# Layer B's transform of time split as 64 by 32, with square transposes on VectorE and matrix products in parts of the array, in a four-layer FFT kernel

## The chip, the cores and the metric

The kernel runs on one core of one Trainium2 chip. The metric is the device time of one whole execution in microseconds. The kernel before was run three times: median 890.2 us, from 884.12 to 890.73.

## The reference

The state `x` has 2048 rows (time `l`) of 512 channels (`d`), float32. Two kinds of layers follow each other, A, B, A, B, each adding to `x` what it makes of the row-normed `x` (LayerNorm without weights).

```python
def A(x, w_r, w_i):                       # a filter in the 2-D spectrum
    X = rfft2(x, axes=(-2, -1))           # 2048 x 512
    return irfft2(X * (w_r + 1j * w_i), s=(2048, 512))

def B(u, A_re, ..., log_dt, Dskip):       # a causal convolution over time, per channel
    dt = exp(log_dt)[:, None]
    P = exp((dt * (A_re + 1j * A_im))[:, :, None] * l)     # 512 x 128 x 2048
    K = einsum("dn,dnl,dn->dl", C, P, dt * Bc).real        # kernel: 512 x 2048
    y = irfft(rfft(u.T, 4096) * rfft(K, 4096))[:, :2048]   # zero-padded
    return y.T + u * Dskip

x = x + A(norm(x)); x = x + B(norm(x)); x = x + A(norm(x)); x = x + B(norm(x))
```

The weights of the two layers A are the same, and so are those of the two layers B, so the kernel `K` and its spectrum are made once.

## The kernel before

Everything is float32 matrix products with tables of sines and cosines, apart from parts of the making of `K`. `x` stays in SBUF as 128 partitions of 16 rows; partition `p` holds rows `16p` to `16p+15`.

**The planner.** Each piece of work is a Python generator (`forward_b`, `group_b`, and so on). A `yield` names the engine and the buffers that the next instructions need and the marks that must have been set. `Clock` simulates the engines with a table of costs (`COST`), takes the ready piece of the lowest rank, and so writes one static order for each engine. Ranks are in the plans `plan_k`, `plan_a` and `plan_rest`. There are two runs of the planner: the first holds the making of `K` and the first layer A, the second all that follows.

**Layer A** is four steps: `forward_a` (norm L505 or L507, sums on POOL L531, products L546 and following, copy), the groups `first_a` and `group_a` in the spectrum (loads of `G`, products, weights), `inv_a` (products L724, copy, product L733, copy, sums on POOL and DVE L744 to L754, new row statistics), and `spread` (ACT square root L490, DVE reciprocal L492), which hands the statistics of four rows on.

**Layer B, before.** The transform of 4096 points is odd-frequency (it carries the zero padding), and splits time as 128 by 16: a product over the 128 partitions, then small transforms over 16. `forward_b` works on two of the 16 rows and half of the channels (`e`): a norm on DVE (L507), eight products with the table `Rb` (L774), two copies on ACT (L776), and a DMA from SBUF to SBUF (L792) that puts the 32 columns of a group beside each other in `place`. `group_b` does one of 16 groups: it loads the kernel's spectrum `khat` (L858) or makes it from `yk`, takes the small transform by products (L804, L805, 32 records), multiplies complex numbers on DVE (L867, twice 128x512) and POOL (L873, twice 128x256), turns back by products (L880), and copies on ACT (L886). `inv_b` moves the rows back by DMA (L895), does the product over time with `RbT` (L902), adds to `x` on DVE (L908), and then either takes the row statistics (L916, L918) or stores a piece of the output (L924, on ACT's queue). In the plan, layer B's forward pieces stand among the inverse pieces of the layer A ahead of it, and layer A's forward pieces among the last pieces of layer B.

**The kernel `K`, before.** `unit_k` builds it 16 channels at a time in 32 units; its last products (L1088) leave 128x256 in PSUM, and two DVE copies (L1099) put them into `KS`. `store_k` writes `KS` to DRAM, `turn_k` reads it back transposed, takes the product over time (L1132), copies on ACT (L1137) and writes `yk`; `spectra_k` makes half of the spectra ahead of layer B, and `group_b` the other half on its first pass.

## Time and profile before

| | |
|---|---|
| median of 3 runs | 890.2 us |
| profiled execution: its span | 887.0 us |
| PE (matrix products) busy | 691.0 us, 78% of the span |
| DVE busy | 565.2 us, 64% |
| ACT busy | 429.1 us, 48% |
| POOL busy | 372.6 us, 42% |
| DMA | 138.22 MB, 156 GB/s in the mean |

The profiled execution is one execution; its span runs from its first to its last instruction, 3.2 us less than the median of the runs.

How to read it: a row of the groups names line, engine, operation, `out<-in` by the program's names, partitions x elements, and a count, then the busy time, the mean of one in ns, and the idle time just before them with what ended it. For a PE row, `128*32` is the part of the array, rows by columns, that a product uses. A product of two float32 operands is two records (`x2048` records are 1024 products). PEld are the loads of the stationary operand, which run beside the products. A row of the timeline has a start in us, a duration, an engine, what it did, and in brackets the idle time before it with what ended that.

### The profile page before, as it was taken

How to read it: one execution, taken by the hardware profiler on the slowest of the kernel's cores; microseconds unless marked ns; L12 is line 12 of the kernel's file. 1: busy time of each engine (PE TensorE's matmuls, PEld its weight loads, DVE VectorE, ACT ScalarE, POOL GpSimd, SP SyncE). 2: the span in 40 equal slices, each digit the busy share in tenths (PEclk: the TensorE clock that was granted, in tenths of full speed). 3: DMA queues.
4: the chain of work that ended last, by engine and by line, in shares of the span. 5: the costliest groups of instructions: out<-in, count | busy, mean ns of one | idle time of the engine just before them, and what ended most of it. 6: DMA issues, size and time to landing. Idle time of an engine off the chain costs nothing. (4 is left out here: it accounts for less than half of the span.)

```text
span 887.0 us, 18504 instructions
## 1 busy us (share of the span) xinstructions
PE 691.0 (78%) x7208; PEld 478.4 (54%) x7208; DVE 565.2 (64%) x1086; ACT 429.1 (48%) x805; POOL 372.6 (42%) x419
## 2 busy tenths in 40 slices
PE   0048767978999888846899989799877897499967
PEld 0046554746666543425556755688755454266746
DVE  6988787546948587692444544586876888265522
ACT  2447677477777867644244213165542454122110
POOL 0047655235536466560234215164443645065430
PEclk9999789979999798988899989799999999799998
DMA  9043003523523844568978993810641067747938
GB/s 332 21 147 95 13 27 130 160 79 110 154 83 114 301 146 144 191 232 175 243 189 239 265 357 124 195 37 15 237 168 42 22 155 186 211 122 186 263 94 226
DMA packets 91862, 138.22 MB, mean 156 GB/s; under 512 B 6812, under 2 KB 61344, under 8 KB 91136
## 3 DMA queue, kind: packets, MB, share of 16 engines
q1 hardware_dynamic: 59520, 107.68, 41.0%
q10 hardware_dynamic: 32256, 29.37, 11.6%
q8 instruction: 57, 0.93, 0.4%
q14 instruction: 29, 0.24, 0.1%
HBM read 76.34 MB, written 27.13 MB: 117 GB/s over the span
## 5 line engine op out<-in xcount | busy, mean ns | idle before, releaser
L873 POOL TENSOR_TENSOR wk<-wk 128x256 f32<-128x256 f32 x128 | 89.2, 727 | 172.9 <-DVE wk L867 169.7
L867 DVE TENSOR_TENSOR wk<-ps,wk 128x512 f32<-128x512 f32 x128 | 79.8, 684 | 91.3 <-PE ps L805 47.3
L1075 POOL TENSOR_TENSOR Y<-wk,Y 128x1024 f32<-128x1024 f32 x32 | 77.0, 2406 | 84.1 <-ACT wk L1063 57.3
L774 PE MATMUL ps<-wk,cRb 128*64 128x256 f32 x512 | 67.7, 406 | 23.1 <-DVE wk L507 23.1
L902 PE MATMUL ps<-wk,cRbT 64*128 64x256 f32 x512 | 68.2, 411 | 15.7 <-DMA wk<-Ya 13.4
L880 PE MATMUL ps<-wk,Y 64*128 64x256 f32 x512 | 73.6, 405 | 2.9 <-POOL wk L873 2.9
L546 PE MATMUL ps<-cRa,wk 128*128 128x128 f32 x128 | 27.6, 300 | 56.9 <-POOL wk L531 56.9
L902 PEld LDWEIGHTS ps<-wk,cRbT 64*128 64x128 f32 x512 | 55.4, 203 | 27.7 <-issue 14.2
L774 PEld LDWEIGHTS ps<-wk,cRb 128*64 128x64 f32 x512 | 46.0, 146 | 44.9 <-DVE wk L507 23.1
L776 ACT COPY wk<-ps 128x512 f32<-128x512 f32 x64 | 37.4, 586 | 62.8 <-PE ps L774 52.6
L531 POOL TENSOR_TENSOR wk<-wk 128x256 f32<-128x256 f32 x32 | 25.0, 780 | 89.3 <-DVE wk L507 55.3
L880 PEld LDWEIGHTS ps<-wk,Y 64*128 64x128 f32 x512 | 43.8, 185 | 32.9 <-POOL wk L873 25.4
L1060 DVE SCALAR_TENSOR_TENSOR wk<-wk,ps 128x1024 f32<-128x1024 f32 x32 | 38.8, 1212 | 33.0 <-ACT wk L1058 33.0
L908 DVE TENSOR_TENSOR x<-x,ps 128x256 f32<-128x256 f32 x64 | 24.8, 408 | 54.6 <-PE ps L902 54.4
L507 DVE TENSOR_SCALAR wk<-x,mv,rs 128x256 f32<-128x256 f32 (+1 forms) x80 | 40.9, 550 | 22.4 <-issue 12.5
L1028 PE MATMUL ps<-wk,Y 96*128 96x512 bf16 x128 | 44.1, 425 | 13.5 <-DVE Y L1071 7.7
L546 PEld LDWEIGHTS ps<-cRa,wk 128*128 128x128 f32 x128 | 21.5, 208 | 58.9 <-POOL wk L531 58.0
L1044 ACT ACTIVATE Y<-ps 128x1024 f32<-128x1024 f32 x48 | 46.9, 1030 | 9.8 <-PE ps L1028 9.1
L1088 PE MATMUL ps<-Y 128*32 128x64 f32 x2048 | 41.9, 244 | 10.1 <-POOL Y L1076 8.2
L1088 PEld LDWEIGHTS ps<-Y 128*32 128x32 f32 x2048 | 36.3, 126 | 24.8 <-POOL Y L1076 13.5
L886 ACT COPY Ya<-ps 128x256 f32<-128x256 f32 x64 | 20.5, 376 | 57.5 <-PE ps L880 55.1
L1071 DVE TENSOR_TENSOR Y<-ps,Y 128x1024 f32<-128x1024 f32 x32 | 39.0, 1218 | 13.5 <-ACT ps L1064 13.5
(218 smaller groups left out, 1802.4 us busy)
## 6 DMA issues: line engine op xcount, KB each, us to landing
wk<-khat SPq DMA_DIRECT2D x48, 256.0 KB, 3.0
yk<-wk ACTq DMA_DIRECT2D x32, 256.0 KB, 3.3
wk<-yk SPq DMA_DIRECT2D x32, 256.0 KB, 3.9
khat<-wk ACTq DMA_DIRECT2D x32, 256.0 KB, 5.4
Y<-in_cGb_dram SPq DMA_DIRECT2D x32, 256.0 KB, 6.0
wk<-Y SPq DMA_DIRECT2D x16, 512.0 KB, 8.9
wk<-Ya SPq DMA_DIRECT2D x16, 512.0 KB, 4.6
Y<-in_W_dram SPq DMA_DIRECT2D x12, 515.0 KB
```

The costliest lines, as they stand in the source:

```text
L507: self.nc.vector.tensor_scalar(xn, self.x[:, s2, d], m, r, op0=OP.subtract, op1=OP.mult)
L546: nc.tensor.matmul(o, pq[:, 0, :], self.Ra, start=True, stop=False)
L774: self.nc.tensor.matmul(p[64 * s:64 * s + 64, 256 * h:256 * h + 256], self.Rb[:, 2 * h + j, :], xn[s], start=True, stop=True)
L867: nc.vector.tensor_tensor(t[c], X[:, c, None, :].to_broadcast([128, 2, 256]), k, op=OP.mult)
L873: nc.gpsimd.tensor_tensor(Z[:, c], t[0][:, c], t[1][:, c], op=op)
L880: nc.tensor.matmul(v[j], gi[o, 2 + c, :], Z[o, c, :], start=c == 0, stop=c == 1)
L902: nc.tensor.matmul(q[s], self.RbT[o, i, :], y[o, i, :], start=i == 0, stop=i == 3)
L1028: self.nc.tensor.matmul(p, f[:, c:c + 128], self.oh[:k, o:o + 512], start=True, stop=True)
L1044: nc.scalar.activation(m[:, :, 1024:] if i == 2 else m[:, i, :1024], p.rearrange("p (i m) -> p i m", i=2) if i == 2 else p, AF.Exp)
L1071: nc.vector.tensor_tensor(E[:, 1, :1024], p, m[:, :1024], op=OP.mult)
L1075: nc.gpsimd.tensor_tensor(E[:, 0, :1024], c, m[:, :1024], op=OP.mult)
L1088: nc.tensor.matmul(pk[32 * j:32 * j + 32, 64 * e:64 * e + 64], E1[:, r, i, :], E2[:, r, i], start=r == 0, stop=r == 1)
```

## The change

Layer B's time is split as 64 by 32 in place of 128 by 16. `x` now has partition `64h + p` hold rows `32p + 16h` to `32p + 16h + 15`, so each load of `x` and each store is two DMAs of 64 partitions (`lines`).

- `norm_b`: the 16 norms of a layer B are on ACT (L497, 128x512), into `Ya`; `NORMS` puts those of the second layer A there too.
- `forward_b`, 16 pieces of 32 channels: two products (L781) that use 64 rows of the array each, then one DVE transpose in squares of 32 by 32 (L784, 128x1024, from PSUM) that writes into `P` the order that the DMA made before.
- `step_b`, 16 pieces in place of 32 of `group_b`: in the first layer a load of `yk` (L808), the kernel's spectrum (16 products, L792), a copy on ACT (L814) and a store of `khat` (L815), in the second layer a load of `khat` (L804); then the spectrum (16 products on 64 rows by 32 columns, L792), a product on DVE of 128x1024 (L825), a copy on ACT of 128x512 (L828), a product on POOL of 128x1024 (L832), 32 products on 32 rows by 64 columns (L840, eight parts of the array), which also do the sums that POOL did before, and two copies on ACT (L846).
- `inv_b`, 8 pieces of 64 channels: a DVE transpose 128x2048 in SBUF (L855), four products of 512 columns (L861), one addition of 128x1024 on DVE (L866). The output leaves in 8 DMAs of 512 KB with runs of 512 bytes on SP's queue (L871). `stats_b` holds the row statistics.
- `rows_k`, 8 pieces, replaces `store_k`, `turn_k` and `spectra_k`: an addition of `Dskip` on POOL, two times four products (L1079) and a transpose (L1083), a store of 1 MB. In `unit_k` one copy on ACT (L1061) replaces the two copies of L1099.
- The plan has four runs, one per layer (`stage`), with buffers and PSUM banks of their own. Layer B's forward pieces no longer stand among layer A's inverse, nor layer A's forward among layer B's end.

```diff
--- before.py
+++ after.py
@@ -11,38 +11,36 @@
+RINGB1 = {"pk": (1024, 3), "kh": (1024, 3), "t0": (1024, 2), "t1": (1024, 2), "xi": (512, 2)}
+RINGB2 = {"kh": (1024, 6), "t0": (1024, 2), "t1": (1024, 2), "xi": (512, 2)}
+RINGP = {"iy": (2048, 4)}
+BANKSB = {'u': (0, 2), 'v': (4, 6)}
...
-NORMS = False, False, True, False
+NORMS = False, True, True, True
...
@@ -759,169 +751,139 @@
-    def turn_b(self, xn, y, kinds):
-    def forward_b(self, r, b, e, st):
-    def rows(self, b, e):
-    def spectra_k(self, q):
-    def tables(self, r):
-    def group_b(self, r, q, e):
-    def inv_b(self, r, b, e, st=None):
...
+    def norm_b(self, r, s2, st):
+        yield "ACT", self.after((id(st), s2 // 4))
+        self.norm(s2, st, self.xn[:, s2, :])
+        self.mark("norm_b", r)
+    def forward_b(self, r, i):
+        nc = self.nc
+        yield "PE p:u", self.after(("norm_b", r), 16)
+        p = self.psum("u")
+        for h in range(2):
+            o = slice(64 * h, 64 * h + 64)
+            nc.tensor.matmul(p[:, 512 * h:512 * h + 512], self.Rb[o, :], self.xn[o, :, 32 * i:32 * i + 32], start=True, stop=True)
+        yield "DVE"
+        e, o = i // 8, 32 * (i % 8)
+        nc.vector.transpose(self.P[:, e, :, o:o + 32].rearrange("p k d -> p d k"), p.rearrange("p (s d) -> p d s", s=32))
+        self.mark("rows", r, e)
+    def spectrum(self, X, g, rows):
+        for r in range(2):
+            for j in range(4):
+                for a in range(2):
+                    self.nc.tensor.matmul(X[32 * j:32 * j + 32, 512 * a + 256 * r:512 * a + 256 * r + 256],
+                                          self.Gb[64 * a:64 * a + 64, 4 * g + j, 32 * r:32 * r + 32], rows(slice(64 * a, 64 * a + 64), j),
+                                          start=True, stop=True)
+    def step_b(self, r, e, g):
+        nc = self.nc
+        k = self.khat[e, g]
+        if r:
+            yield "SP kh"
+            kh = self.w("kh", [128, 2, 2, 256])
+            nc.sync.dma_start(kh.rearrange("p a r d -> p (a r d)"), k)
+        else:
+            yield "SP pk", self.after("rows_k", 8)
+            y = self.w("pk", [128, 4, 4, 64])
+            nc.sync.dma_start(y.rearrange("p b k d -> p b (k d)"), self.yk[4 * e:4 * e + 4, :, 256 * g:256 * g + 256].rearrange("b p m -> p b m"))
+            yield "PE p:u kh", self.after("tables"), self.emitted("turn", 8 * e + g)
+            K, kh = self.psum("u"), self.w("kh", [128, 2, 2, 256])
+            self.spectrum(K, g, lambda o, j: y[o, :, j, :])
+            self.mark("turn")
+            yield "ACT"
+            nc.scalar.copy(kh.rearrange("p a r d -> p (a r d)"), K)
+            nc.scalar.dma_start(k, kh.rearrange("p a r d -> p (a r d)"))
+            self.drop(y, K)
+        yield "PE p:u", self.after(("rows", r, e), 8), self.emitted(("step", r), 8 * e + g)
+        X = self.psum("u")
+        self.spectrum(X, g, lambda o, j: self.P[o, e, 4 * g + j, :])
+        self.mark("step", r)
+        X = X.rearrange("p (a r d) -> p a r d", a=2, r=2)
+        yield "DVE t0"
+        four = [128, 2, 2, 256]
+        t0 = self.w("t0", four)
+        nc.vector.tensor_tensor(t0, X[:, :, 0, None, :].to_broadcast(four), kh, op=OP.mult)
+        yield "+ACT xi"
+        xi = self.w("xi", [128, 2, 256])
+        nc.scalar.copy(xi, X[:, :, 1, :])
+        self.timer.drop(X)
+        yield "POOL t1"
+        t1 = self.w("t1", four)
+        nc.gpsimd.tensor_tensor(t1, xi[:, :, None, :].to_broadcast(four), kh[:, :, ::-1, :], op=OP.mult)
+        self.drop(xi)
+        yield "PE p:v p:v"
+        v = [self.psum("v") for _ in range(2)]
+        for n, (t, c, b) in enumerate(((t0, 0, 0), (t0, 1, 2), (t1, 0, 1), (t1, 1, 2))):
+            for i in range(4):
+                o = slice(32 * i, 32 * i + 32)
+                for a in range(2):
+                    nc.tensor.matmul(v[i // 2][64 * a:64 * a + 64, 512 * (i % 2):512 * (i % 2) + 256], self.Ib[o, g, a, b, :], t[o, a, c, :],
+                                     start=n == 0, stop=n == 3)
+        self.drop(t0, t1, kh)
+        yield "ACT"
+        for i in range(2):
+            k1 = 4 * g + 2 * i
+            nc.scalar.copy(self.P[:, e, k1:k1 + 2, :], v[i].rearrange("p (i d) -> p i d", i=2)[:, :, :256])
+            self.drop(v[i])
+        self.mark("grouped", r, e)
+    def inv_b(self, r, e, i, st=None):
+        nc = self.nc
+        yield "DVE iy", self.after(("grouped", r, e), 8), self.emitted(("rows", r, 1), 8)
+        y = self.w("iy", [128, 32, 64])
+        nc.vector.transpose(y.rearrange("p s d -> p d s"), self.P[:, e, :, 64 * i:64 * i + 64].rearrange("p k d -> p d k"))
+        yield "PE p:v"
+        q = self.psum("v")
+        for c in range(2):
+            for h in range(2):
+                o = 16 * h + 8 * c
+                nc.tensor.matmul(q[64 * h:64 * h + 64, 512 * c:512 * c + 512], self.RbT, y[:, o:o + 8, :], start=True, stop=True)
+        self.drop(y)
+        yield "DVE"
+        d = 256 * e + 64 * i
+        xs = self.x[:, :, d:d + 64]
+        nc.vector.tensor_tensor(xs, xs, q.rearrange("p (s d) -> p s d", s=16), op=OP.add)
+        self.mark("added_b", r, e)
+        if st is None and i % 2:
+            yield "SP"
+            for of, to in self.lines("out", slice(0, 16), slice(d - 64, d + 64)):
+                nc.sync.dma_start(to, of)
+    def stats_b(self, e, i, st):
...
@@ -1087,60 +1051,40 @@
-        yield "DVE", self.emitted("kernel", u)
-        o = 4 * (u % 8)
-        k = pk[:, :256].rearrange("p (e h k) -> p e h k", e=4, h=2)
-        for h, l in enumerate((slice(32, 64), slice(31, None, -1))):
-            nc.vector.tensor_copy(KS[u // 8][:, l, o:o + 4].rearrange("p l e -> p e l"), k[:, :, h])
+        yield "ACT", self.emitted("kernel", u)
+        o = 4 * (u % 4)
+        nc.scalar.copy(KS[b][:, :, o:o + 4, :], pk[:, :256].rearrange("p (e h k) -> p h e k", e=4, h=2))
         self.mark("kernel")
...
-    def store_k(self, q, KS):
-    def turn_k(self, q, i):
...
+    def rows_k(self, b, KS):
+        nc = self.nc
+        yield "POOL", self.after("kernel", 4 * b + 4)
+        o = KS[b][:, 1, :, 0]
+        nc.gpsimd.tensor_tensor(o, o, self.Dk[:, 16 * b:16 * b + 16], op=OP.add)
+        K = KS[b].rearrange("p h d s -> p h (d s)")
+        for a in range(2):
+            yield "PE p:a" if a else "PE p:a T"
+            if a == 0:
+                T = self.w("T", [128, 32, 64])
+            p = self.psum("a")
+            for h in range(2):
+                for j in range(2):
+                    o = slice(64 * a + 32 * j, 64 * a + 32 * j + 32)
+                    nc.tensor.matmul(p[:, 512 * j:512 * j + 512], self.Rk[o, h, :], K[o, h, :], start=h == 0, stop=h == 1)
+            if a:
+                self.drop(KS[b])
+            yield "DVE"
+            nc.vector.transpose(T[:, :, 32 * a:32 * a + 32].rearrange("p k d -> p d k"), p.rearrange("p (d s) -> p d s", s=32))
+            self.drop(p)
+        yield "SP"
+        nc.sync.dma_start(self.yk[b], T.rearrange("p k d -> p (k d)"))
+        self.mark("rows_k")
...
@@ -1152,43 +1096,37 @@
+        self.stage(BANKS1, SAME1, self.plan_a(st), (RING, self.Y), (RING0, self.Y), (RINGX, self.x.rearrange("p s d -> p (s d)")),
+                   (RINGW, self.wk), (RING1, self.wk[:, n:]))
+        self.stage(BANKSB, {}, self.plan_b(0, st[1], st[2]), (RINGB1, wk), (RINGP, self.Ya))
+        self.stage(BANKSA, {}, self.plan_a2(st[2], st[3]), (RINGG, self.Y[:, 8192:]), (RINGA, self.Ya), (RINGC, wk))
+        self.stage(BANKSB, {}, self.plan_b(1, st[3]), (RINGB2, wk), (RINGP, self.Ya))
...
@@ -1245,12 +1169,25 @@
...
+    def plan_b(self, r, st, sn=None):
+        if r == 0:
+            yield 0, self.tables()
+        for s2 in range(16):
+            yield s2, self.norm_b(r, s2, st)
+        for i in range(16):
+            yield 20 + i, self.forward_b(r, i)
+        for e in range(2):
+            for g in range(8):
+                yield 40 + 8 * e + g, self.step_b(r, e, g)
+            for i in range(4):
+                yield 40 + 8 * (e + 1) + 2 * i, self.inv_b(r, e, i, sn)
+            if sn is not None:
+                for i in range(4):
+                    yield 60 + i, self.stats_b(e, i, sn)
```

The rest of the diff are the tables for the new split (`tables_b`, `host_k`, `cH`), loads of `x` by `lines`, the mirrored half of `E` in `unit_k`, and a cost for products in parts of the array in the planner.

The planner's order shows the change best in the second layer B. On PE, before, from the last forward products to the end of the layer; L804 and L805 alternate until the products of a first group come in between (`Rb` is the forward table, `ps` PSUM, `wk` and `Y` work buffers):

```order
L774 MATMUL ps<-wk,cRb 64x256 x32
L804 MATMUL ps<-Y 64x256
L805 MATMUL ps<-Y 64x256
...
L880 MATMUL ps<-wk,Y 128x256 x4
...
L880 MATMUL ps<-wk,Y 128x256 x8
L902 MATMUL ps<-wk,cRbT 128x256 x64
```

On PE, after, from the end of layer A to the first steps, and the end of the layer:

```order
L725 MATMUL ps<-wk,cRaT 128x512 x2
L781 MATMUL ps<-Ya,cRb 128x512 x32
L792 MATMUL ps<-Y,wk 32x256 x64
L840 MATMUL ps<-wk 64x256 x32
L792 MATMUL ps<-Y,wk 32x256 x16
...
L840 MATMUL ps<-wk 64x256 x128
L861 MATMUL ps<-Ya,cRbT 64x512 x16
```

All 32 forward products now stand in a row behind layer A, four spectra are taken ahead of the first products of a step, and then one spectrum and one step's products alternate; at the end the products of the last four steps stand ahead of the last four inverse pieces.

On ACT, after, at the start of the same layer (`rs` and `nb` are the rows' scale and bias, `mv` their statistics, `Ya` the normed rows):

```order
L728 COPY wk<-ps 128x512
L738 COPY wk<-wk 128x2
L482 ACTIVATE rs<-mv,eps 128x4
L497 ACTIVATE Ya<-x,nb,rs 128x512 x16
L828 COPY wk<-ps 128x512 x3
L846 COPY Y<-ps 128x512 x2
```

The 16 norms stand behind the last square root of layer A, where before they stood on DVE in pairs among the row statistics and additions of layer A's inverse, of which this is the end:

```order
L482 BN_STATS st<-x 128x6
L483 BN_AGGR mv<-st 128x2
L492 RECIPROCAL rs<-rs 128x2
L507 TENSOR_SCALAR wk<-x,mv,rs 128x256 x4
L867 TENSOR_TENSOR wk<-ps,wk 128x512 x40
L908 TENSOR_TENSOR x<-x,ps 128x256 x2
```

On DVE, after, the same place:

```order
L484 RECIPROCAL rs<-rs 128x4
L487 SCALAR_TENSOR_TENSOR nb<-mv,rs 128x4
L784 STREAM_TRANSPOSE Y<-ps 128x32x32 x16
L825 TENSOR_TENSOR wk<-ps,wk 128x1024 x10
L855 STREAM_TRANSPOSE Ya<-Y 128x64x32 x2
L866 TENSOR_TENSOR x<-x,ps 128x16x64
```

The 16 forward transposes stand in a row between layer A's last statistics and the first product of a step, and the transposes of the inverse among and behind the steps.

392 lines of the change are left out of this document (104 added, 288 removed).

## The prediction

> **What bounds the kernel now.** I read first the busy time by stage, with the span cut where the work changes hands: at 400.5 us the last row statistics of the first layer A are done, at 606 the second layer A has finished its forward products, at 697 its inverse starts, at 756.5 its last statistics are done. Columns: window, its length, then busy us (instructions) of PE, PE weight load, DVE, ACT, POOL; granted clock, DMA share, GB/s.
>
> ```profile
> 80.00:400.50 320.50, 257.51 (x3609) 166.94 (x3609) 229.90 (x372) 223.70 (x303) 169.43 (x134) 0.90 0.41 130
> 400.50:606.00 205.50, 181.01 (x1348) 130.24 (x1345) 101.44 (x215) 75.24 (x171) 68.08 (x98) 0.92 0.72 197
> 606.00:697.00 91.00, 72.65 (x730) 57.29 (x729) 62.71 (x166) 39.52 (x137) 39.95 (x56) 0.98 0.33 113
> 697.00:756.50 59.50, 51.15 (x567) 29.83 (x566) 53.38 (x120) 31.03 (x70) 29.74 (x38) 0.97 0.58 147
> 756.50:887.00 130.50, 104.61 (x800) 72.98 (x800) 53.31 (x102) 23.21 (x69) 44.43 (x64) 0.93 0.68 182
> ```
>
> The two layers B (second and last row) are PE's: 88% and 80% busy, nothing else above half. The first stage has no single owner (PE 80%, DVE 72%, ACT 70%). The inverse of the second layer A is DVE's (53.4 of 59.5). Then the chain that ended last shows what interrupts PE in the last layer B: the moves that turn rows by DMA (start, us, what).
>
> ```profile
> 758.33 8.90 DMA Y<-wk
> 767.22 4.87 issue
> 858.26 4.61 DMA wk<-Ya
> 863.01 10.04 PE ps L902 x64
> 873.07 7.92 DMA wk<-Ya
> ```
>
> 26 us of that layer are these moves; the rest is matrix work.
>
> **The change, part by part.** The rows that give the prices (group; busy us, mean ns of one; idle before):
>
> ```profile
> L1088 PE MATMUL ps<-Y 128*32 128x64 f32 x2048 | 41.9, 244 | 10.1 <-POOL Y L1076 8.2 <-ACT wk L658 0.8 <-ACT wk L746 0.5
> L1075 POOL TENSOR_TENSOR Y<-wk,Y 128x1024 f32<-128x1024 f32 x32 | 77.0, 2406 | 84.1 <-ACT wk L1063 57.3 <-issue 26.1 <-POOL Y L1076 0.6
> L1071 DVE TENSOR_TENSOR Y<-ps,Y 128x1024 f32<-128x1024 f32 x32 | 39.0, 1218 | 13.5 <-ACT ps L1064 13.5
> L776 ACT COPY wk<-ps 128x512 f32<-128x512 f32 x64 | 37.4, 586 | 62.8 <-PE ps L774 52.6 <-DMA Y<-wk 10.1
> L1132 PE MATMUL ps<-wk,cRk 128*128 128x512 f32 x64 | 31.3, 611 | 3.2 <-DVE wk L1124 1.4 <-ACT wk L821 1.1 <-ACT Y L1044 0.7
> L804 PE MATMUL ps<-wk 128*64 128x256 f32 x128 | 23.3, 437 | 8.2 <-DMA wk<-in_cGk_dram 4.2 <-DVE Y L1071 3.3 <-ACT wk L821 0.7
> L805 PE MATMUL ps<-wk 128*64 128x256 f32 x128 | 22.9, 418 | 2.0 <-issue 2.0
> L1099 DVE COPY wk<-ps 128x128 f32<-128x128 f32 x64 | 19.3, 376 | 24.5 <-PE ps L1088 20.4 <-ACT wk L1058 2.5 <-issue 1.6
> L1137 ACT COPY wk<-ps 128x512 f32<-128x512 f32 x32 | 18.8, 588 | 14.1 <-PE ps L1132 6.3 <-DVE wk L745 2.7 <-DMA yk<-wk 1.8
> L821 ACT COPY wk<-ps 128x512 f32<-128x512 f32 x16 | 9.3, 584 | 5.8 <-PE ps L805 5.8
> L952 DVE TENSOR_TENSOR Y<-Y 128x2048 f32<-128x2048 f32 x2 | 4.6, 2276 | 0.8 <-ACT Y L950 0.8
> L637 DVE TENSOR_TENSOR Y<-Y,ps 128x128 f32<-128x128 f32 x12 | 3.5, 288 | 7.3 <-ACT Y L635 7.0
> ```
>
> *Products in parts of the array.* No product of the change's shape (64 rows by 32 columns, 32 by 64; eight parts at once) is in the trace. An f32 product is two records. Quarter-wide products start four records every 0.107 us, and PE stands still when the shape of the parts changes:
>
> ```profile
> 723.33 0.27 PE L724 MATMUL ps<-cDaT,apart 128*32 128x128 f32 x1
> 723.44 0.27 PE L724 MATMUL ps<-cDaT,apart 128*32 128x128 f32 x1
> 783.82 0.20 PEld L804 LDWEIGHTS ps<-Y 128*64 128x64 f32 x4 [0.33 <-issue]
> 787.47 0.30 PEld L880 LDWEIGHTS ps<-wk,Y 64*128 64x128 f32 x4 [0.39 <-POOL wk L873]
> 815.56 2.00 PE ps L902 x16
> ```
>
> Four records of 128 columns in 0.107 us are 26.7 ns each, 0.83 ns per column in each part; eight parts with 256 columns would again be 26.7 ns per record if all eight run together, and 53 ns if only four do. L1088 sets another floor: 41.9 us over 2048 records is 20.5 ns where four parts of 64 columns need 13.3, so a 32-column weight load takes up to 0.64 ns per column; 64 columns 41 ns. A step's product (32 products, 64 records) then costs 1.7 us (all hidden) to 2.6 (weights) to 3.4 (four parts); I take 2.3, between the first two. A spectrum (16 products, 32 records, 32-column weights) costs 0.85 to 1.0 to 1.7; I take 1.0. The Trainium skill (TensorE: Matmul & The Clock Gate, Part 3) gives 3.07 times for four row parts and 10.6 for sixteen parts; by that, an estimate of 5.7 for eight (0.71 of eight, the mean of both) would make these 2.4 and 1.2 and the time some 12 us longer, and no run here shows it.
>
> A step is then spectrum 1.0, change of shape 0.39, product 2.3, change 0.33, about 4.0 us; X's buffer comes free a little late (VectorE starts when half the product has read its tile: 0.1), so 4.2. The next product may start when ScalarE has emptied both tiles `v` (2 copies of 0.59 and two hops of 0.2 = 1.6 us): hidden under spectrum and changes. POOL's 2.41 and DVE's 1.22 per step lie beneath. In the first layer a step also has the kernel's spectrum: 1.0 more, and 0.6 every second step where two spectra share a buffer: 5.3.
>
> *Square transposes.* 16 per layer of 128x1024 from PSUM, 8 of 128x2048 in SBUF. Without a penalty for writing single 4-byte elements a kilobyte apart, L1071 and L952 price them: 1.22 and 2.28 us. L1099 writes such elements: 376 ns, against 288 for L637 of the same size. If those 88 ns are per element (0.69 ns), the prices are 1.93 and 3.7. But two L1099 in a row take 0.58 us:
>
> ```profile
> 387.31 0.58 DVE L1099 COPY wk<-ps 128x128 f32<-128x128 f32 x2
> ```
>
> The second adds 0.20 us, which is 128 elements at DVE's usual 1.05 ns plus 0.07; so most of the excess is paid once per instruction. I take 1.4 and 2.5 and keep both ends. A rule of the Trainium skill speaks against the change here: SBUF is reached in lines of 16 bytes and each crossing to a new line pays (SBUF — State Buffer, Specifications (TRN2)); both transposes cross at every element, and the pair above shows little of it.
>
> *Queues.* SP issues, at the end of the first stage, the last store of `rows_k` (1 MB), the two tables of layer B (2.5 MB, into the room of that stage's `T`) and the loads of `yk`. At the 197 GB/s that the first layer B moves now, 5 MB to the first three `pk` take 25 us; the first kernel spectrum is due 36 us after that stage, so they are hidden, and late by their own excess if they are not. Behind a load that waits for its buffer stand the tables of the next layer A, which are due only after 26 us of its forward products. In the last layer the first two pieces of output stand before the last load of `khat` on SP; that load is due four steps later.
>
> *The ends of a layer.* All 16 norms now come on ACT behind the last square root, before the first product; last statistics, then:
>
> ```profile
> 756.59 0.30 ACT L490 ACTIVATE rs<-mv,eps 128x2 f32<-128x2 f32 x1 [0.37 <-DVE mv L483]
> 756.92 0.17 DVE L492 RECIPROCAL rs<-rs 128x2 f32<-128x2 f32 x1 [0.36 <-ACT rs L490]
> 568.60 2.22 ACT L505 ACTIVATE wk<-x,nb,rs 128x512 f32<-128x512 f32 x3 [0.44 <-DVE nb L495]
> 569.55 0.73 POOL L531 TENSOR_TENSOR wk<-wk 128x256 f32<-128x256 f32 x1 [16.70 <-ACT wk L505]
> 570.92 0.73 POOL L531 TENSOR_TENSOR wk<-wk 128x256 f32<-128x256 f32 x1
> 563.30 0.43 DVE L916 BATCH_NORM_STATS2 hm<-x 128x6 f32<-128x256 f32 x1
> 563.76 0.21 DVE L918 BATCH_NORM_AGGREGATE mv<-hm 128x2 f32<-128x12 f32 x1
> q10 hardware_dynamic: 32256, 29.37, 11.6%
> ```
>
> Spread 1.4 us; norms 16 x 0.74 = 11.9; first product 1.2 (half of L902's 2.00, which is 16 records of 256 in two row halves, and a hop); 15 transposes until the buffer for the first spectrum is free, 21.0; from there to the end of the first product 7 (change 0.39, spectrum 1.0, copy 0.8, POOL 2.4, hops, product 2.3); 15 steps; four inverse products of the first half, 4 x (1.93 + two changes 0.75) = 10.8; after the last product two copies 1.4, then four transposes and two additions on DVE (4 x 2.5 + 2 x 1.22 = 12.4), a last product 2.1 and a last addition 1.5 = 17.4.
>
> Second layer B: 1.4 + 11.9 + 1.2 + 21 + 7 + 15 x 4.2 + 10.8 + 17.4, and the output: 2048 packets of 512 bytes over 16 engines, at about 35 ns (queue q10: 11.6% of 16 x 887 us over 32256 packets is 51 ns for 910 bytes) plus 2, 6.5: **140 us for 130.5, a loss of 9.7**.
>
> First layer B, to the end of the next layer's forward products: 1.4 + 11.9 + 1.2 + 21 + 10 (three kernel spectra come first) + 15 x 5.3 + 10.8 + 17.4, statistics 16 x (0.46 + 0.12) = 9.3, then layer A's forward without the overlap it has now, norm 0.8, POOL 16 x 1.4, 3.3 of drain = 26.5: **189 for 205.5, a gain of 16.5**. Its DMAs, 1 MB per step of 5.3 us, ask for 198 GB/s where that window moves 197 now: hidden, with three buffers ahead.
>
> Inverse of the second layer A: layer B's norms and products leave it. The two windows' rows for L774 (PE) and L507 (DVE):
>
> ```profile
> 697.00:756.50 59.50, 29.51 (x224) 17.83 (x224) 0.97 0.58 147
> 697.00:756.50 59.50, 14.68 (x28) 0.97 0.58 147
> ```
>
> DVE bounds it and loses 14.7 us: **gain 14**.
>
> First stage: three quarters of L1132 (23.4) and half of L804 and L805 (23.1) leave PE; 16 pieces of `rows_k` come, each like L902's 16 records: 16 x 1.93 = 31; net 15.6 less. ACT loses 14.1 of L1137 and L821's 9.3, and gains 32 copies for L1099 at 0.38, 12: 11 less, its DMA issues beside. DVE swaps 19.3 for 16 x 1.4 = 22. Between nothing (a chain through DVE paces it) and 30 (PE paces it, with its stalls): **gain 15**.
>
> Sum: 887.0 - 15 - 16.5 - 14 + 9.7 = 851 of span; the median of the runs, 890.2 (884.1 to 890.7), lies 3.2 above the profiled span of 887.0: **854 us**. The runs spread by 0.75%, so 1% is what can be told from no change.
>
> **Rivals.** *The array runs four parts at once, not eight* (slower). For: no row shows more than four. Against: four run without loss. The product is then 3.4 and the spectrum 1.7: per step 1.1 + 1.4 = 2.5 more in the first layer, 1.8 in the second, 16 x 4.3 = 69: 923. It decides against the change from 44 ns per record (3584 records x 10 ns = 36 us). *Transposes cost L1099's excess on every element* (no change): 15 x 0.53 in each forward part, 4 x 1.2 in each tail, 4 in the first stage: 16 + 10 + 4 = 30: 884. For: the line rule of the Trainium skill above. Against: the pair. If those in SBUF also wait for POOL, 10 more. *All at the cheap ends* (faster still): first stage 28, transposes 1.22 (6), product 1.7 and spectrum 0.85 (16 x 0.9 + 16 x 0.75 = 26): 854 - 13 - 32 = 809; half of it 830. *The first stage doesn't shorten*: 869. That the change doesn't do what it says is no case: in its order of instructions every DMA between forward and inverse is gone.
>
> **How the numbers follow.** Forecast with its near cases (835 to 875) 0.45; four to five parts 0.22; dear transposes 0.17; faster still 0.16. Faster by over 1% (below 881): 0.44 of the forecast, 0.16, and 0.03 of the dear transposes, 0.63; within 1%: 0.01 + 0.02 + 0.11 = 0.14; slower 0.20 + 0.03 = 0.23. The range reaches from the half of the cheap ends, with some of what lies below it, to the first rival: 815 to 923.
>
> **What would show it.** Right: steps of 4.2 us in the last layer and 5.3 in the first, PE its bound; records about 36 ns apart in the product; a 0.39 stall at each change of shape; transposes of 1.4 and 2.5; no DMA between forward and inverse; the second layer A's inverse near 45 us; the last layer B longer than now. Wrong: records 44 ns or more apart, transposes near 2 and 4 us, steps paced by ScalarE's copies, or a first stage that still ends at 400.

## The result, and the profile after

The changed kernel takes 896.15 us (median of 16 runs, 890.69 to 901.69), the kernel before 886.51 us in the 16 runs beside it: a ratio of 1.0107 with a 95% interval of 1.0083 to 1.0132, about 1% slower where 4% faster was forecast. The profiled execution has a span of 899.5 us against 887.0.

The stages of the profile after, cut at the same events as those of before (window, its length, busy us of PE, weight loads, DVE, ACT, POOL, then granted clock, DMA share, GB/s):

```profile
80.00:400.80 320.80, 255.75 (x3547) 160.00 (x3545) 250.70 (x320) 211.27 (x295) 174.61 (x142) 0.87 0.20 68
400.80:598.80 198.00, 135.53 (x2364) 73.29 (x2364) 125.15 (x138) 76.53 (x132) 61.31 (x50) 0.88 0.35 122
598.80:679.75 80.95, 64.59 (x528) 53.08 (x526) 55.98 (x151) 33.35 (x123) 32.51 (x45) 0.94 0.36 126
679.75:735.00 55.25, 36.23 (x545) 19.15 (x544) 48.83 (x105) 20.45 (x53) 37.37 (x48) 0.88 0.04 11
735.00:899.50 164.50, 98.57 (x1664) 43.33 (x1664) 89.73 (x50) 37.07 (x65) 37.73 (x16) 0.83 0.28 75
```

| stage | before | forecast | after | pairs alone (below) |
|---|---|---|---|---|
| to the end of the first layer A | 400.5 | 385.5 | 400.8 | 397.1 |
| first layer B and forward products of the second A | 205.5 | 189 | 198.0 | 179.8 |
| groups of the second A | 91.0 | 91 | 81.0 | 79.7 |
| inverse of the second A | 59.5 | 45.5 | 55.3 | 54.9 |
| second layer B | 130.5 | 140 | 164.5 | 138.2 |
| span | 887.0 | 851 | 899.5 | 849.7 |

The second layer B misses most, by 24.5 us; there DVE is busy for 89.7 us, where before it was for 53.3. The DMAs between forward and inverse are gone, as forecast, and the DMA share of that stage falls from 0.68 to 0.28. What stands in their place shows in the groups:

```profile
L855 DVE STREAM_TRANSPOSE Ya<-Y 128x2048 f32<-128x2048 f32 x16 | 67.2, 4239 | 19.3 <-ACT Y L846 19.3
L784 DVE STREAM_TRANSPOSE Y<-ps 128x1024 f32<-128x1024 f32 x32 | 55.7, 1865 | 26.3 <-PE ps L781 26.3
L1083 DVE STREAM_TRANSPOSE wk<-ps 128x1024 f32<-128x1024 f32 x16 | 31.2, 1952 | 34.6 <-PE ps L1079 19.2 <-ACT Y L1006 10.2 <-issue 5.2
L840 PE MATMUL ps<-wk 32*64 32x256 f32 x2048 | 74.4, 402 | 14.1 <-POOL wk L832 5.3 <-ACT Y L846 4.9 <-DVE wk L825 3.0
L792 PE MATMUL ps<-Y,wk 64*32 64x256 f32 x1024 | 37.4, 402 | 18.8 <-ACT wk L828 17.2 <-DVE Y L784 1.3 <-ACT wk L814 0.3
L861 PE MATMUL ps<-Ya,cRbT 128*64 128x512 f32 x128 | 43.5, 815 | 33.6 <-DVE Ya L855 29.2 <-ACT Y L846 4.4
```

The products came out as priced: L840's 74.4 us over 32 steps is 2.3 us each, and 1.98 in the timeline below. The transposes did not: 1.87 and 1.95 us for 128x1024 where the sum had 1.4, 4.24 us for 128x2048 where it had 2.5. L861 waits 29.2 us for L855.

A step of the second layer B, in the timeline of PE, DVE and ACT (start, us, what, in brackets the idle time before and its releaser):

```profile
784.24 1.10 PE L792 MATMUL ps<-Y,wk 64*32 64x256 f32 x32 [1.25 <-ACT wk L828]
785.26 1.98 PE L840 MATMUL ps<-wk 32*64 32x256 f32 x64
788.50 1.10 PE L792 MATMUL ps<-Y,wk 64*32 64x256 f32 x32 [1.25 <-ACT wk L828]
```

```profile
786.55 1.23 DVE L825 TENSOR_TENSOR wk<-ps,wk 128x1024 f32<-128x1024 f32 x1 [3.04 <-PE ps L840]
```

```profile
787.86 0.58 ACT L828 COPY wk<-ps 128x512 f32<-128x512 f32 x1 [2.70 <-DVE wk L825]
```

From one spectrum (784.24) to the next (788.50) are 4.26 us, nearly the 4.2 of the forecast, but otherwise made up: spectrum and product are 3.0, no stall stands at the change of shape, and PE idles 1.25 us for the spectrum's PSUM buffer. That buffer is free when ScalarE has copied `xi`; `xi` (787.86) starts when `t0` (786.55) has ended, and `t0` waits for the product that frees one of its two buffers.

### The profile page after: what moved, and what is told of

It is laid out like the page before. It is cut to its first block, busy times and chain, and to the rows that moved or that the text cites. A ratio compares the mean times of both kernels' runs of the same rounds, so it can differ in the third digit from the quotient of the medians.

```text
span 899.5 us, 20702 instructions
## 1 busy us (share of the span) xinstructions
PE 614.6 (68%) x8808; PEld 369.7 (41%) x8808; DVE 634.3 (71%) x878; ACT 415.0 (46%) x721; POOL 364.7 (41%) x331
## 3 DMA queue, kind: packets, MB, share of 16 engines
q8 instruction: 69, 1.13, 0.5%
## 5 line engine op out<-in xcount | busy, mean ns | idle before, releaser
L832 POOL TENSOR_TENSOR wk<-wk 128x1024 f32<-128x1024 f32 x32 | 75.6, 2365 | 200.0 <-ACT wk L828 200.0
L825 DVE TENSOR_TENSOR wk<-ps,wk 128x1024 f32<-128x1024 f32 x32 | 39.2, 1224 | 79.5 <-PE ps L840 34.5
L840 PE MATMUL ps<-wk 32*64 32x256 f32 x2048 | 74.4, 402 | 14.1 <-POOL wk L832 5.3
L855 DVE STREAM_TRANSPOSE Ya<-Y 128x2048 f32<-128x2048 f32 x16 | 67.2, 4239 | 19.3 <-ACT Y L846 19.3
L781 PE MATMUL ps<-Ya,cRb 64*128 64x512 f32 x128 | 40.3, 718 | 56.0 <-ACT Ya L497 40.7
L828 ACT COPY wk<-ps 128x512 f32<-128x512 f32 x32 | 18.7, 585 | 126.2 <-DVE wk L825 126.2
L784 DVE STREAM_TRANSPOSE Y<-ps 128x1024 f32<-128x1024 f32 x32 | 55.7, 1865 | 26.3 <-PE ps L781 26.3
L861 PE MATMUL ps<-Ya,cRbT 128*64 128x512 f32 x128 | 43.5, 815 | 33.6 <-DVE Ya L855 29.2
L523 POOL TENSOR_TENSOR wk<-wk 128x256 f32<-128x256 f32 x32 | 25.1, 784 | 95.3 <-DVE wk L499 55.3
L840 PEld LDWEIGHTS ps<-wk 32*64 32x64 f32 x2048 | 45.1, 137 | 42.6 <-ACT Y L846 15.3
L1083 DVE STREAM_TRANSPOSE wk<-ps 128x1024 f32<-128x1024 f32 x16 | 31.2, 1952 | 34.6 <-PE ps L1079 19.2
L1006 ACT ACTIVATE Y<-ps 128x1024 f32<-128x1024 f32 x48 | 47.2, 1037 | 10.2 <-PE ps L990 9.4
L725 PE MATMUL ps<-wk,cRaT 128*128 128x512 f32 x64 | 39.9, 718 | 15.8 <-ACT wk L720 10.8
L792 PE MATMUL ps<-Y,wk 64*32 64x256 f32 x1024 | 37.4, 402 | 18.8 <-ACT wk L828 17.2
L846 ACT COPY Y<-ps 128x512 f32<-128x512 f32 x64 | 34.7, 593 | 27.3 <-PE ps L840 26.5
```

The costliest lines, as they stand in the source:

```text
L784: nc.vector.transpose(self.P[:, e, :, o:o + 32].rearrange("p k d -> p d k"), p.rearrange("p (s d) -> p d s", s=32))
L792: self.nc.tensor.matmul(X[32 * j:32 * j + 32, 512 * a + 256 * r:512 * a + 256 * r + 256], self.Gb[64 * a:64 * a + 64, 4 * g + j, 32 * r:32 ...
L825: nc.vector.tensor_tensor(t0, X[:, :, 0, None, :].to_broadcast(four), kh, op=OP.mult)
L832: nc.gpsimd.tensor_tensor(t1, xi[:, :, None, :].to_broadcast(four), kh[:, :, ::-1, :], op=OP.mult)
L840: nc.tensor.matmul(v[i // 2][64 * a:64 * a + 64, 512 * (i % 2):512 * (i % 2) + 256], self.Ib[o, g, a, b, :], t[o, a, c, :], start=n == 0, ...
L855: nc.vector.transpose(y.rearrange("p s d -> p d s"), self.P[:, e, :, 64 * i:64 * i + 64].rearrange("p k d -> p d k"))
```

## The experiments

Two theories stood at first for the transposes. *Far elements*: each 4-byte element that is read or written alone, hundreds of bytes from the next, costs extra (elements that follow each other are called near or flat below). *The operation's own rate*: a square transpose takes 1.8 to 2.1 ns per element whatever the layout. A third, that the loss lay elsewhere (clock, steps), was open as well. The kernels of one group ran beside the kernel before on the same chip; ratios are to it. All edits are to the changed kernel.

**1. Transposes that read and write one element after the other.** Of the three lines, the first:

```diff
-nc.vector.transpose(self.P[:, e, :, o:o + 32].rearrange("p k d -> p d k"), p.rearrange("p (s d) -> p d s", s=32))
+nc.vector.transpose(self.P[:, e].rearrange("p k d -> p (k d)")[:, 32 * o:32 * o + 1024], p)
```

> The changed kernel with its three transposes (L784, L855, L1083) reading and writing one element after the other instead of elements 128 to 1024 bytes apart; the values land in other places, so layer B computes something else, with the same work. Theory, far elements: a transpose is dear because its elements lie apart, so now it takes 1.2 to 1.3 us for 128x1024 and 2.2 to 2.4 for 128x2048, and the time falls by 40 to 60 us, to some 845. Rival, the operation's own rate: 1.86, 1.95 and 4.24 us stay, whatever the layout, and the time stays within 1% of 896.

845.58 us, ratio 0.9536 (0.9496 to 0.9576): 50 us less than the changed kernel.

```profile
L784 DVE STREAM_TRANSPOSE Y<-ps 128x1024 f32<-128x1024 f32 x32 | 38.9, 1241 | 28.7 <-PE ps L781 28.0
L855 DVE STREAM_TRANSPOSE Ya<-Y 128x2048 f32<-128x2048 f32 x16 | 36.0, 2286 | 3.0 <-ACT Y L846 3.0
L1083 DVE STREAM_TRANSPOSE wk<-ps 128x1024 f32<-128x1024 f32 x16 | 19.9, 1244 | 35.2 <-PE ps L1079 18.2 <-ACT Y L1006 11.8 <-issue 5.2
```

The same instructions take 1.24 and 2.29 us. So 1.86, 1.95 and 4.24 are not the operation's own rate; the layout is the price, and turned flat it gives back 50 us, more than the 42 us that the change missed its forecast by.

**2. Plain copies, far and near.** `transpose` replaced by `tensor_copy`, once with the patterns of the change, once with those of experiment 1 (the first of three lines each).

```diff
-nc.vector.transpose(self.P[:, e, :, o:o + 32].rearrange("p k d -> p d k"), p.rearrange("p (s d) -> p d s", s=32))
+nc.vector.tensor_copy(self.P[:, e, :, o:o + 32].rearrange("p k d -> p d k"), p.rearrange("p (s d) -> p d s", s=32))
```

```diff
+nc.vector.tensor_copy(self.P[:, e].rearrange("p k d -> p (k d)")[:, 32 * o:32 * o + 1024], p)
```

> The changed kernel with plain copies on VectorE in place of the three transposes, with the very same reading and writing patterns; nothing is turned between partitions, so layer B computes something else. Far elements: 1.9 us and 4.2 us as now, no change of the time. The operation's own rate: 1.2 us and 2.3 us, and the time falls by 40 to 60 us.

> Plain copies that read and write one element after the other, in place of the transposes; layer B computes something else. Both theories: 1.2 us and 2.2 us. It measures what the price of the transposes is worth in the whole time: 15 x 0.65 in each forward part, 2 us in each of 16 transposes of the inverse, and up to 12 us in the first stage, together 40 to 60 us, so some 845. If the loss against the forecast lies elsewhere (the clock, the steps), the time stays above 875.

Far: 876.37 us, ratio 0.9871 (0.9813 to 0.9929). Near: 836.84 us, ratio 0.9433 (0.9393 to 0.9474).

```profile
L784 DVE COPY Y<-ps 128x1024 f32<-128x1024 f32 x32 | 55.4, 1875 | 26.1 <-PE ps L781 26.1
L855 DVE COPY Ya<-Y 128x2048 f32<-128x2048 f32 x16 | 40.5, 2559 | 19.1 <-ACT Y L846 19.1
L1083 DVE COPY wk<-ps 128x1024 f32<-128x1024 f32 x16 | 30.8, 1923 | 36.2 <-PE ps L1079 18.8 <-ACT Y L1006 12.1 <-issue 5.2
```

From PSUM a far copy costs what the transpose costs (1.88 against 1.87, 1.92 against 1.95), so it is not the turning. From SBUF neither expectation held, and the means of L855 (2.56 us far, 1.88 near) mix two cases, as single copies show (the first three rows from the near kernel, the last from the far one):

```profile
482.25 2.35 POOL L832 TENSOR_TENSOR wk<-wk 128x1024 f32<-128x1024 f32 x1 [5.24 <-ACT wk L828]
482.54 3.14 DVE L855 COPY Ya<-Y 128x2048 f32<-128x2048 f32 x1
531.18 1.22 DVE L855 COPY Ya<-Y 128x2048 f32<-128x2048 f32 x1
855.14 2.25 DVE L855 COPY Ya<-Y 128x2048 f32<-128x2048 f32 x1
```

Eleven of the 16 near copies take 1.21 to 1.23 us and twelve of the 16 far ones 2.20 to 2.30; the nine others, 3.07 to 4.17 us, all began while POOL was at its product L832. So in SBUF a far copy pays about 1.03 us for 2048 elements, half of the transpose's 1.95, and the near copy alone takes about half of the near transpose's 2.29. What makes the copy cheaper is not settled.

**3. Which side pays.** Far writes with near reads, then near writes with far reads (of L784 and L855; L1083 reads near in the change already). The edit of L784 in the one and in the other:

```diff
+nc.vector.transpose(self.P[:, e, :, o:o + 32].rearrange("p k d -> p d k"), p.rearrange("p (d s) -> p d s", s=32))
```

```diff
+nc.vector.transpose(self.P[:, e].rearrange("p k d -> p (k d)")[:, 32 * o:32 * o + 1024].rearrange("p (d k) -> p d k", k=32),
+                    p.rearrange("p (s d) -> p d s", s=32))
```

> The changed kernel with the reads of the transposes L784 and L855 made one element after the other, the writes left as they are (L1083 is so already); layer B computes something else. Writes pay: 1.86 us for 128x1024 as now, and 128x2048 between 3.5 and 4.24. Reads pay: 1.24 and 2.3 us, L1083 apart.

> The same with the writes of all three transposes one element after the other, and the reads of L784 and L855 as far apart as now; layer B computes something else. Writes pay: 1.24 us and 2.3 us, and the time is that of all flat, about 846. Reads pay: 1.86 us and above 3.5.

One run each, 880.27 and 869.05 us. Far writes:

```profile
L784 DVE STREAM_TRANSPOSE Y<-ps 128x1024 f32<-128x1024 f32 x32 | 55.7, 1863 | 26.5 <-PE ps L781 26.5
L855 DVE STREAM_TRANSPOSE Ya<-Y 128x2048 f32<-128x2048 f32 x16 | 58.3, 3726 | 0.0
```

Far reads:

```profile
L784 DVE STREAM_TRANSPOSE Y<-ps 128x1024 f32<-128x1024 f32 x32 | 38.9, 1240 | 28.6 <-PE ps L781 28.0
L855 DVE STREAM_TRANSPOSE Ya<-Y 128x2048 f32<-128x2048 f32 x16 | 58.7, 3691 | 19.3 <-ACT Y L846 19.3
```

Reading PSUM 128 bytes apart is free (1.24). Writing SBUF far costs 0.62 us per 1024 elements (1.86 against 1.24), 0.61 ns each. In SBUF both sides pay, 1.40 for the reads and 1.44 for the writes of 2048 (3.69 and 3.73 against 2.29), and together 1.95 (4.24 in the change). "Writes pay" was half of the truth.

**4. The wait in the step.** A third `t0`, with one `pk` and one `kh` less, and `xi` issued first:

```diff
+        yield "ACT xi"
+        xi = self.w("xi", [128, 2, 256])
+        nc.scalar.copy(xi, X[:, :, 1, :])
-        yield "DVE t0"
+        yield "+DVE t0"
...
-        yield "+ACT xi"
-        xi = self.w("xi", [128, 2, 256])
-        nc.scalar.copy(xi, X[:, :, 1, :])
```

> The changed kernel with a third buffer t0 (the loads give up one buffer in each layer) and with ScalarE's copy xi issued ahead of VectorE's product t0. Theory: a step of 4.26 us is a ring of spectrum 1.03, half a product 1.1, t0 1.23 and xi 0.58, since t0 waits for the product that reads the last but one and the spectrum's buffer is free only after xi; without the two waits it is 3.2 to 3.4 us, PE's 3.0 and the wait for v. 15 x 0.9 in the last layer, half of that in the first: the time falls by 15 to 25 us. Rival, the single pair of v: the next product waits for the two copies of v at once, so a step stays above 3.8 and the time falls by less than 8 us.

872.92 us, ratio 0.9838 (0.9801 to 0.9874), 23 us less.

```profile
769.24 1.09 PE L792 MATMUL ps<-Y,wk 64*32 64x256 f32 x32
770.27 2.19 PE L840 MATMUL ps<-wk 32*64 32x256 f32 x64
772.39 1.09 PE L792 MATMUL ps<-Y,wk 64*32 64x256 f32 x32
```

A step is now 3.1 us (772.39 - 769.24), PE without a gap. The single pair `v` holds nothing up, as the prediction had it. What each of the two edits gave was not measured apart.

**5. Layout by elements, the far side moved to other engines.** On top of 4, `P` is laid out channel by channel, so that VectorE's transposes are near on both sides:

```diff
-        self.P = self.Y.rearrange("p (e k d) -> p e k d", e=2, k=32)
+        self.P = self.Y.rearrange("p (e d k) -> p e k d", e=2, k=32)
...
-        y = self.w("iy", [128, 32, 64])
+        y = self.w("iy", [128, 64, 32])
```

> The kernel with the third t0 and xi first (872.9 us), its layout turned so that L784 and L855 read and write one element after the other; it computes the reference's result. What was far moves to others: the spectrum's products read their rows 128 bytes apart, the copies of v on ScalarE write elements 128 bytes apart, the addition reads PSUM 64 bytes apart. If far elements cost only on VectorE's transposes: 1.24 and 2.3 us, and 30 to 40 us less, 833 to 843. If TensorE pays for far rows: the spectrum doubles to 2 us, 32 us are given back, and the time is 865 or more. If ScalarE pays per element as VectorE does (0.6 ns, 0.3 us a copy): a step stays near 3.1 to 3.5 and the time below 855.

889.5 us, ratio 1.0002 (0.9973 to 1.0031): slower than 4 by 17 us.

```profile
L792 PE MATMUL ps<-Y,wk 64*32 64x256 f32 x1024 | 93.2, 872 | 7.4 <-DVE wk L828 7.1 <-DVE Y L784 0.2
L846 ACT COPY Y<-ps 128x512 f32<-128x512 f32 x64 | 61.6, 1065 | 65.5 <-PE ps L840 65.5
L784 DVE STREAM_TRANSPOSE Y<-ps 128x1024 f32<-128x1024 f32 x32 | 38.5, 1237 | 28.9 <-PE ps L781 27.9
L866 DVE TENSOR_TENSOR x<-x,ps 128x1024 f32<-128x1024 f32 x16 | 19.2, 1208 | 12.6 <-PE ps L860 10.4 <-ACT wk L824 2.1
```

TensorE and ScalarE pay too, TensorE more than the expected 2 us. The spectrum's products, which read their moving rows 128 bytes apart, are busy 93.2 us for 37.4 (2.95 us for 1.10 in the timeline), and ScalarE's copies, which write 128 bytes apart, take 1065 ns for 593. The addition L866 reads PSUM 64 bytes apart at no cost (1208 for 1219 of after). Moving a far access in SBUF to another engine bought nothing here.

**6. Norms earlier.** On top of 4, the norms of the second layer B behind each group of four statistics, in the inverse of layer A, then also the writes of L855 near (`iy` by channels, the product reads runs of 16), then the norms of the first layer B in two halves of the channels. Each kernel adds one of these to the one before it. The edits in `plan_a2`, `inv_b` and `plan_b`:

```diff
+            yield 91 + s2, self.norm_b(1, s2, sa)
...
-        nc.vector.transpose(y.rearrange("p s d -> p d s"), self.P[:, e, :, 64 * i:64 * i + 64].rearrange("p k d -> p d k"))
+        nc.vector.transpose(y, self.P[:, e, :, 64 * i:64 * i + 64].rearrange("p k d -> p d k"))
...
+            yield s2, self.norm_b(r, s2 % 16, st, slice(256 * (s2 // 16), 256 * (s2 // 16) + 256))
```

> The kernel with the third t0 and xi first (872.9 us), and the 16 norms of the second layer B issued in the inverse of the second layer A, each group of four behind its own statistics. Theory: 12 of the 16 norms then lie under work that VectorE bounds, so that 9 to 10 us go, to about 863. Rival: ScalarE's copies in that inverse are on its chain, and the norms between them give the gain back: 870 or more.

> The kernel with the third t0, xi first and early norms (863.5 us), with only the writes of the inverse's transpose L855 made one element after the other: its buffer iy is laid out channel by channel, the product over time reads runs of 16 elements, and the far elements are left to the addition, which reads them from PSUM. It computes the reference's result. Theory: far reads from SBUF stay (3.7 us for 4.24), far reads from PSUM cost nothing (the addition stays at 1.22), runs of 16 elements cost TensorE nothing: 0.55 in each of the 16 transposes, 12 to 16 of them on the path, 7 to 9 us, to about 856. Rival: TensorE pays for the runs (each run starts anew), the four inverse products go from 1.94 to 3 or more, and the time is 863 or more.

> The same, and the norms of the first layer B in two halves of the channels, the first products behind the first half. Theory: 16 norms of 128x256 take some 7.5 us in place of 12.5, the other half lies under the transposes: 4 to 5 us less than the kernel with the turned buffer iy alone. Rival: the second half ends after the eighth transpose and nothing is won; by 8 x 1.73 = 14 us of transposes it should not.

863.54 us (ratio 0.9719, 0.9667 to 0.9771), 857.7 (0.9673, 0.9611 to 0.9735), 849.79 (0.9566, 0.9512 to 0.9621). The first did what it should, 9.4 us; the second gave some 6 where 7 to 9 were expected, the third 8 for 4 to 5, both within what the runs scatter (855 to 862 and 843 to 851). L855 is at 3702 ns; the products that read runs of 16 elements are busy 39.0 us, 40.6 without that edit, so they pay nothing.

**7. Pairs.** On top of `iy` by channels, two rows `k` beside each other, so that a far access is a run of 8 bytes:

```diff
-        self.P = self.Y.rearrange("p (e k d) -> p e k d", e=2, k=32)
+        self.P = self.Y.rearrange("p (e h d k) -> p e h k d", e=2, h=16, k=2)
```

> The kernel with the turned buffer iy, with pairs of rows in place of single ones in the layout between the transposes: L784 writes and the inverse's transpose reads runs of 8 bytes, the spectrum's products read elements 8 bytes apart, the copies of v write one after the other. It computes the reference's result. If each line of 16 bytes that is touched costs, pairs pay half of the excess: L784 about 1.55 us (1.86 and 1.24 are the ends), the inverse's transpose about 3.0 (3.7 and 2.3), and the spectrum, two elements of four in each line, twice 1.1 or less (2.95 where the elements lay 128 bytes apart). If only a distance above some bytes costs: 1.24, 2.3 and 1.1, and the time falls by 30 us.

One run, 826.63 us, 31 less.

```profile
L784 DVE STREAM_TRANSPOSE Y<-ps 128x1024 f32<-128x1024 f32 x32 | 38.4, 1232 | 20.9 <-PE ps L781 19.6
L854 DVE STREAM_TRANSPOSE Ya<-Y 128x2048 f32<-128x2048 f32 x16 | 36.5, 2294 | 14.2 <-ACT Y L845 14.2
L792 PE MATMUL ps<-Y,wk 64*32 64x256 f32 x1024 | 36.6, 391 | 5.2 <-DVE wk L828 5.0 <-DVE Y L784 0.2
```

Pairs do not pay half, they pay nothing: 1.23 and 2.29 us as with flat layouts, though the runs lie 2 KB apart. The spectrum, whose rows now lie 8 bytes apart, is at 391 ns a record (402 in the change), the copies, which write one after the other, at 592. The Trainium skill (SBUF — State Buffer, Specifications (TRN2)) has lines of 16 bytes and asks for at least two accesses to a line for full bandwidth; a pair is two, and the trace agrees (1.23 us with pairs, 1.87 with single elements). The expectation had made of the lines a price for each one touched.

**8. Pairs alone, and all together.** To see whether the price of single far elements alone made the miss, the changed kernel with `iy` by channels, pairs in all layouts (`rows_k` and its `yk` too) and nothing else; then all edits of 4, 6 and 7 with it. The edit in `rows_k`:

```diff
-                T = self.w("T", [128, 32, 64])
+                T = self.w("T", [128, 16, 64, 2])
```

> The changed kernel (896.2 us) with nothing but its layouts turned to pairs: all three transposes write runs of 8 bytes or one after the other, and read pairs or PSUM; two t0, xi behind t0 and late norms stay as they are. It computes the reference's result. If the price of single far elements is what the forecast missed, the time is that of the transposes with flat reads and writes, 845.6, within 6 us, and VectorE's transposes take 1.24 and 2.29 us everywhere. Rival: the pairs won their 31 us only together with the other edits (the step without waits), since the transposes hid other waits: 865 or more here.

> All edits together: pairs in all three layouts, the third t0, xi first, early norms in the second layer B and norms in two halves in the first. It computes the reference's result. Against the one look at pairs with the other edits (826.6 us): the first stage's transposes at 1.24 for 1.95 end that stage 5 to 10 us earlier, as all-flat transposes did (390.9 for 400.8), and the halves take 5 to 8 us: about 812. If another engine paces the end of the first stage, 820.

Pairs alone: 850.23 us, ratio 0.9572 (0.9529 to 0.9614). All: 812.09 us, ratio 0.9148 (0.9074 to 0.9222). Pairs alone:

```profile
L784 DVE STREAM_TRANSPOSE Y<-ps 128x1024 f32<-128x1024 f32 x32 | 38.4, 1232 | 28.4 <-PE ps L781 27.0
L854 DVE STREAM_TRANSPOSE Ya<-Y 128x2048 f32<-128x2048 f32 x16 | 36.3, 2292 | 16.6 <-ACT Y L845 16.6
L1082 DVE STREAM_TRANSPOSE wk<-ps 128x1024 f32<-128x1024 f32 x16 | 20.0, 1247 | 41.3 <-PE ps L1078 25.9 <-ACT Y L1005 10.2 <-issue 5.2
```

The rival, that the pairs gain only with the other edits, falls. The last layer B with pairs alone is 138.2 us where 140 was forecast. With all edits the time is as expected, but not its parts: the first stage ends at 396.7 us, 3 earlier than in experiment 7 (400.0) and not 5 to 10.

## Why the prediction was wrong, point by point

**The step that failed** is "Square transposes": "most of the excess is paid once per instruction. I take 1.4 and 2.5". It is paid on every element: 1.87 us in place of 1.4, 4.24 in place of 2.5. The quoted pair of L1099 said so: its second copy took 0.07 us more than 128 elements at the usual rate. That is 0.55 ns per element, 0.56 us on 1024, and with the 1.22 us of L1071 would have given 1.78 for the 1.87 measured. The excess looked small because the instruction was; the division was not made. For L855 neither end held (2.28 to 3.7, measured 4.24): the row that priced the upper end wrote far and read near, and the transpose in SBUF does both.

**What it was worth.** Between the change and pairs alone only layouts differ, and of the other rows none grew (spectrum 400 ns for 402, copies 594 for 593, addition 1207 for 1219). So the price of single elements, with the waits that hang on it, is 896.2 - 850.2 = 46 us, and at 1.24 and 2.29 for the assumed 1.4 and 2.5 the kernel is 4 us from the forecast of 854. Partly by luck: in the table the first stage and the inverse of the second A are 21 us above their terms, the first layer B and the groups 20 below. The case that came is the rival of dear transposes, 884, or 894 with the wait for POOL. It had the right mechanism at too small a size: 4.24 for 3.7 in 16 transposes adds 9 to its 884, 893 for the 896 measured. Its chance of 0.17 came from that same misread pair. The wait for POOL did not come: the five L855 beside a POOL product took 4.24 to 4.41 us, the eleven others 4.15 to 4.26.

**Products in parts of the array**: right. 1.98 us for 64 records is 31 ns each, between the ends for eight at once (1.7) and weights (2.6), and far from the 44 ns from which four at a time would have decided.

**The step**: 4.26 for 4.2 and, in the first layer, two steps in 10.2 us for 2 x 5.3, right in sum and wrong in parts. The stalls at changes of shape (0.72) did not come; the wait for the buffer, costed at 0.1, was 1.25. Experiment 4, which takes the wait away and finds no stall under it, separates them. The two rows that priced the stalls, 0.33 and 0.39 us, were of the weight loads, and POOL's product ended the second; PE's own rows at the same times show no idle time before them:

```profile
783.82 0.66 PE L804 MATMUL ps<-Y 128*64 128x256 f32 x4
787.47 1.18 PE L880 MATMUL ps<-wk,Y 64*128 64x256 f32 x8
```

**The ends of the last layer**: norms with the spread 11.6 for 13.3, output 8.7 for 6.5, about right. The 15 forward transposes took 26.3 us for 21.0; the rest is in the inverse, whose transposes L855 set the pace between the halves and at the end. There PE, which waits for them, is also granted less clock (last section): the mean of this layer is 0.83, and 0.91 with pairs alone.

**First stage**: the gain of 15 did not come (400.8 for 400.5). The case named for its lower end did, a chain through DVE. In the last 60 us DVE is busy throughout, where before it had gaps; first before, then after:

```profile
340.00:400.50 60.50, 42.08 (x653) 23.14 (x647) 49.06 (x96) 36.25 (x61) 39.48 (x41) 0.86 0.55 181
```

```profile
340.00:400.80 60.80, 37.52 (x592) 20.38 (x592) 60.11 (x94) 28.36 (x52) 40.42 (x42) 0.80 0.09 36
```

The prediction set 22 us of transposes against 19.3 of L1099; they are 31.2. And the two-operand additions of layer A's inverse grew beside them, in this window from 13.9 us (22 of them) to 20.9 (24). The first of the two lines, before and after, the same code:

```profile
L753 DVE TENSOR_TENSOR x<-x,wk 128x256 f32<-128x256 f32 x11 | 6.7, 611 | 1.2 <-ACT wk L746 1.2
```

```profile
L745 DVE TENSOR_TENSOR x<-x,wk 128x256 f32<-128x256 f32 x12 | 11.4, 949 | 0.0
```

One beside an addition on POOL, and one with POOL idle:

```profile
386.96 1.30 POOL L741 TENSOR_TENSOR x<-x,wk 128x512 f32<-128x512 f32 x1
387.06 1.48 DVE L745 TENSOR_TENSOR x<-x,wk 128x256 f32<-128x256 f32 x1
399.06 0.43 DVE L745 TENSOR_TENSOR x<-x,wk 128x256 f32<-128x256 f32 x1
```

Of the 24, the twelve with no POOL instruction beside them took 0.40 to 0.43 us each, the twelve others 1.33 in the mean and up to 2.52; before, twelve took 0.41 to 0.43 and the ten beside POOL 0.89. So they are slow only beside POOL; no experiment moved POOL's work away. With pairs the stage still ends at 397.1, so the transposes are not all of it. Eight profiles with the same work in that stage as the change end it between 395 and 401, two with pairs at 397, three with flat writes at 390 to 392, though pairs and flat writes cost the same 1.24 us. How much of the 15 each cause holds stays open.

**Second layer A**: the inverse gained 4 us, not 14, and the groups before it 10 that were not forecast: 14.3 together for 14. The sum was right, its place was not; the inverse's additions are again the slower ones (55.3 us with DVE busy 48.8).

**Rivals**: four parts at once did not come. No DMA holds up a step, as the paragraph on queues had it.

## What to carry to other kernels

Divide an excess by the elements that pay it before calling it small, and multiply it by those of the new instruction. A layout that is turned on the way should keep two 4-byte elements beside each other on the SBUF side; the far side belongs in PSUM reads, which were free here. A transpose that replaces a DMA is only off the path where the engine that does it is: here the work went to DVE, which then paced parts of three stages. A mean over a group can mix cases, as the copies of experiment 2 show, and an idle time belongs to the engine of its row: PE's weight loads are not PE.

## What the runs showed of the hardware that was not expected

Single 4-byte elements far apart in SBUF cost on three engines: on VectorE 0.61 to 0.70 ns per element where one side of a transpose is far, 0.95 where both are (0.50 for a plain copy), 0.92 ns on ScalarE's writes ((1065 - 593) / 512), 2.7 times the time on TensorE's moving rows. On VectorE runs of 8 bytes cost none of it, and on TensorE rows 8 bytes apart; ScalarE was not tried with pairs. Products in eighth parts of the array ran at 31 ns per record of 256 columns. VectorE's copies and two-operand additions within SBUF took 1.22 us (128x2048) and 0.41 us (128x256) alone and up to 3.40 and 2.52 beside POOL; the transposes within SBUF did not (4.15 to 4.41 us).

PE that has stood still starts slowly. In the second layer B after the norms (timeline of PE, the first and a later group of the same products):

```profile
746.65 3.78 PE L781 MATMUL ps<-Ya,cRb 64*128 64x512 f32 x8 [19.80 <-ACT Ya L497]
750.73 2.84 PE L781 MATMUL ps<-Ya,cRb 64*128 64x512 f32 x8 [0.29 <-DVE Y L784]
754.52 1.13 PE L781 MATMUL ps<-Ya,cRb 64*128 64x512 f32 x4 [0.95 <-DVE Y L784]
```

The first eight records take 3.78 us, the next eight 2.84, and four later ones 1.13, so 2.26 for eight. The granted clock (the third figure from the end) rises in the same stretches from half to full:

```profile
746.00:750.50 4.50, 3.78 (x8) 1.18 (x8) 1.72 (x1) 0.60 (x1) 0.00 (x0) 0.50 0.00 0
750.50:754.00 3.50, 2.84 (x8) 0.80 (x8) 3.31 (x3) 0.00 (x0) 0.00 (x0) 0.77 0.00 0
754.00:760.00 6.00, 3.73 (x14) 1.21 (x16) 6.00 (x5) 0.00 (x0) 0.00 (x0) 1.00 0.00 0
```

So the products behind a wait of 19.8 us were slow by the clock. In the inverse of the same layer it is 0.50 again behind a wait of 4.9 us for L855 (873 to 877 us), and eight records of L861 take 3.68 us there, 1.94 at full clock (887.62). The mean of the profile is 0.882, of the one before 0.932; no term of the sum had it, and what it costs in all was not measured.
